# The first expert's rows are loaded before the last unit's scatter, and that unit's rows are added in PSUM

## The chip, the cores and the metric

One NeuronCore of a Trainium2 chip runs the whole program as one launch. The metric is the device time of one execution in microseconds; lower is better. Engines: PE (TensorE: products), DVE (VectorE), ACT (ScalarE), POOL (GpSimd, which also issues the indirect DMAs) and SP (SyncE, which issues most DMAs). Each engine works through its own instructions in the order of the program.

## The reference

Three layers in a row, all in float32:

```python
for t in range(768):                    # attention, 4 x 8 heads of width 40
    y[:, :, t] = r_t @ state
    Sa = state @ a_t
    state = state * w_t - outer(Sa, b_t) + outer(v_t, k_t)
x = y as 3072 tokens x 320
expert = argmax(x @ w_gate)             # 8 experts, 3072 / 8 * 2 = 768 rows each at most
gate = softmax(x @ w_gate)[expert]
x = gate * (relu(x_rows @ w1[expert]) @ w2[expert])     # F = 1024
out = elu(x @ w_in) @ w_out             # 2048 wide
```

A token's place in its expert's list is its rank among the tokens of that expert, counted in the order of the tokens.

## The kernel before

**Two halves.** `attention` works through 24 units of 128 tokens (64 steps of two batches). Each unit ends in one block of 128 rows of x, 320 wide. `ffn` follows it, with tile pools of its own in the memory that attention's pools leave: first the eight experts, then six blocks of 512 sorted tokens through the last layer.

**The table between them.** `disp` lies in DRAM: for each expert, 448 rows of 329 numbers (320 of x, the token's number, 8 logits of the gate). It is filled with zeros early. For a unit u the steps at its end are: `x` (line 558: product XT with IW on PE, copy into the tile XO on ACT, logits and token number on DVE), `b` (route: argmax as a 0/1 row, on DVE), `j` (line 592: ranks by two small products on PE, then the row numbers into `slot` on DVE) and `D` (line 609: an indirect DMA from POOL that scatters the 128 rows of XO into `disp`; a small memset follows it).

**The order.** What each engine gets is the order in which the Python program emits it. Attention's steps are generators; each letter of `ORDER`, and of what `slot(k)` returns for the units from 5 on, advances one of them. `V` advances the conversion of the last layer's weights from float64 to float32, in pieces: load on SP, integer and float operations on DVE (lines 858 to 870), store to `w32` on SP. Behind the last slot come, by hand: x and b of unit 23, six products that only keep PE busy (`warm`), j of unit 23, its scatter D, and the rest of V.

**The start of the experts.** `experts` (line 1192) splits the second half of the first expert's weights (`split`, lines 775 and 780: a copy on ACT gives the high part, four products on POOL for each of four quarters give the low part). Then `start` (line 917) loads the rows of expert 0, 448 rows as 112 partitions by 4, with one DMA on SP (line 1087), does 26 busy products, and turns the rows with twelve transposes into three PSUM banks (line 935). `prep` makes the high and low parts XH, XL and XS of them on ACT and DVE (lines 954 and 955). `fetch(2)` then loads the next weights on SP (lines 801 and 803).

**The steps of an expert.** Each expert has 8 steps f of 128 hidden columns. A step is `s1` (line 970: eight products of 448 columns into one of four PSUM banks), `relu` one step later (H on ACT, line 1100, and the remainder L on DVE, line 1101) and `s2` three steps later (lines 1035 to 1045: eight products). Between them, `extra(b, f)` puts other work: a cast of a quarter of later weights on ACT (the next weight load is issued in steps 0 and 4, as soon as the buffer that it refills has been read), conversion pieces with their loads (`more`), the next expert's rows (load in step 0, softmax of the gate in steps 2 and 3, turned in steps 4 to 6), and for expert 0 alone `late_gate` (line 1257). Its gate is worked out from the logits in the loaded rows and laid on the output columns, since the rows are turned without it: softmax before step 0 and in step 2, the products of line 1263 in step 3, a copy in step 4.

Of the kernel before, what the change touches and what calls it, by code (L numbers as in the profile page):

```python
# [33 lines left out]
ORDER = """
se1 sa0 se0 se0 v1 sc0 e0.0 sv se1 e0.1 sd p0 sw p0 e1.0 sw a0 p0 v0 p1 sa1 sx a0 p1 lw sz st1 e2.0 c0.0 a1
p2 p2 a1 c0.0 e1.1 sr1 Z7 c0.1 p1 e3.0 c0.1 k0.0 k0.1 c0.1 c1.0 e2.1 a2 a2 c1.0 p3 c1.1 k1.1 k1.0 c1.1 k1.0 e4.0 d1 k1.1
c1.1 e3.1 m0.0 l0 m0.1 k0.1 p2 p3 a3 l1 a3 p4 p4 p3 m1.1 c2.1 e5.0 k2.1 c2.0 c2.1 m1.0 r0 c2.0 k2.0 k0.0 a4 m2.1 a4 p5
st0 k2.0 k3.1 sc1 c3.0 c2.1 c3.1 ss1 k3.0 e4.1 m2.0 p4 r0 r1 c4.0 i0 e6.0 k3.0 n0 k3.1 m3.0 k4.1 p5 n1 o0 c3.1 p6
c3.0 e5.1 a5 a5 c3.1 m3.1 k2.1 r1 e7.0 l2 p5 k4.1 c4.1 k4.0 m4.1 e6.1 c4.0 c5.1 k5.1 l3 p6 k5.0 c5.0 c4.1 p7 c4.1 p6 a6
m5.0 a6 v2 v3 p7 c5.0 t1 m4.0 t0 c6.1 m6.1 c5.1 k4.0 f1 k6.1 c5.1 k6.0 k6.1 m5.1 sr0 a7 i1 c6.0 f1 f0 a7 o1 e7.1 e8.0 f1 f0  # L40
k5.0 p7 c6.1 f0 f1 f1 p8 c6.0 d0 e9.0 f0 k5.1 c7.1 f0 f1 f1 c6.1 c7.0 f0 f0 e8.1 c7.1 g1 c7.0 g0 p8 m7.0 a8 ss0 p8 m7.1
g0 k7.1 l5 l4 g1 k7.0 k7.1 g0 k8.0 g0 c7.1 l6 p9 e9.1 g1 a8 u0 m6.0 p9 k6.0 k8.1 u0 g1 l7 c8.0 k7.0 m8.0 c8.1 n2 t2 e10
w0 a9 p9 f2 n3 k8.1 a9 q0.0 w0 q0.1 q0.1 w0 i2 u1 u1 f2 q0.0 c8.0 f2 p10 k9.1 c9.1 f2 c8.1 c9.0 m8.1 k8.0 Z2 c8.1 f2 w0
Z4 p10 t3 f2 s0 k9.1 p10 c9.1 c9.0 w1 w1 k9.0 y0 f2 i2 k9.0 g2 s0 w1 e11 s0 c9.1 f3 k10.1 Z3 r2 a10 w1 a10 f3 k10.1 m9.0
f3 y0 m9.1 k10.0 p11 Z0 r2 c10.0 q1.0 q1.0 c10.1 x0 f3 p11 h2 q1.1 s1 f3 g2 a11 k10.0 m10.1 i2 f3 c10.0 g2 q1.1 c10.1 h2
e12 v4 p11 f3 s1 c10.1 x0 y1 y1 d2 g3 p12 a11 s1 k11.1 c11.0 x1 g3 r3 Z6 c11.0 g2 g3 p12 k11.1 h3 x1 m11.0 a12 Z5 p12 x0 r3
u2 a12 c11.1 c12.0 u2 g3 w2 d3 c11.1 w2 k11.0 w2 x1 k12.1 h3 q2.0 q2.1 Z1 b0 w2 c11.1 c12.1 u3 c12.1 m10.0 m11.1 s2 j0
o2 u3 w3 k11.0 q2.1 q3.1 c12.0 e13 z2 q2.0 s2 w3 y2 s2 l11 j0 l10 y2 t4 m12.0 m12.1 r4 v5 l9 g4 d4 w3 k12.1 r4 p13 D0
h4 x2 l8 g4 c12.1 k12.0 D1 h4 t5 q3.0 p13 w3 g4 g4 g4 s3 u4 x2 a13 l12 s3 z3 q3.0 u4 w4 w4 a13 q3.1 p13 i3 w4 g5 h5 y3
d5 x2 w4 y3 s3 s4 i3 k12.0 e14 t6 s4 s4 h5 v6  # L50
"""
FIRST = [f for f, n in GROUPS if f > 6]
AHEAD = (17, 19, 20, 21, 22, 23)

CV0, CVN = 17, 7


def slot(k):
    L = []
    a = lambda x: L.extend(x.split())  # L60
    live = k < NU

    nx, up = k + 1, k + (8 if k < 7 else 9)
    ups = up < NU
    pair = k - 3 if k % 2 else None
    work = {f - 6 + i: (g, i) for g, (f, n) in enumerate(GROUPS) for i in range(4) if f > 8}
    work[5] = (3, 3)
    w = work.get(k)
    if live: a(f"r{k} r{k}")
    if ups and k != 7: a(f"c{up}.0")  # L70
    if FU <= k < NU: a(f"g{k} g{k}")
    more = ups and up + 1 < NU
    if ups and k != 7: a(f"m{up}.0 c{up}.0")
    if more and k != 7: a(f"p{up+1}")
    a(f"x{k-2} x{k-2} x{k-2}")
    if k == NU: a(f"b{NU-2}.1")
    if FU <= k < NU: a(f"g{k} g{k}")
    if w and w[1]:
        a(f"i{w[0]}")
        if w[1] == 3: a(f"o{w[0]}")  # L80
    if k % 2 == 0: a(f"D{k-3}")
    second = f"c{up}.1 m{up}.1 c{up}.1 c{up}.1 p{up+1} l{up}"
    if ups: a(second if k != 7 else f"a{up} a{up} c{up}.0 m{up}.0 c{up}.0 p{up+1}")
    if k + 2 < NU: a(f"v{k+2}")
    V = (lambda: a("V")) if CV0 <= k < NU else (lambda: None)

    if nx in FIRST: a(f"t{nx}")
    a(f"q{k-1}.0 q{k-1}.0")
    V()
    if w and not w[1] and k != 6: a(f"i{w[0]}")  # L90
    if live: a(f"u{k} u{k}")
    if k == 7: a(second)
    if more: a(f"p{up+1}")
    a(f"q{k-1}.1 q{k-1}.1")
    V()
    if pair is not None: a(f"b{pair}")
    if ups:
        a(f"k{up}.0 k{up}.0 k{up}.1 k{up}.1")
    if FU <= nx < NU and nx not in FIRST: a(f"g{nx}")
    if live and k < 22: a(f"w{k} w{k} w{k} w{k}")  # L100
    if up + 2 < NU: a(f"E{up+2}")
    if more: a(f"a{up+1} a{up+1}")
    a(f"z{k-1}")
    if nx < NU: a(f"h{nx} h{nx}")
    if nx < NU: a(f"d{nx}")
    if k + 2 < NU and k + 2 not in FIRST: a(f"t{k+2}")
    if live and k < 22: a(f"s{k} s{k} s{k}")
    if k == NU: a(f"j{NU-2}.1 j{NU-2}.1 D{NU-2}")
    a(f"y{k-1} y{k-1}")
    if nx in FIRST: a(f"g{nx}")  # L110
    V()
    if pair is not None: a(f"j{pair} j{pair} D{pair}")
    if k == 6:
        up += 1
        a(f"c{up}.0 m{up}.0 c{up}.0 c{up}.1 m{up}.1 c{up}.1 c{up}.1 p{up+1} l{up} i{w[0]}")
        a(f"k{up}.0 k{up}.0 k{up}.1 k{up}.1 E{up+2} p{up+1} p{up+1}")
    return " ".join(L)


def attention(tc, nc, e_in, v_tok, d_in, wg, disp, xt, cst, ring, early, early_w, cv, cap):  # L120
# [548 lines left out]
    for k in range(KR, NU + 1):  # L669
        for key in slot(k).split():  # L670
            go(key)
        for _ in range(AHEAD.count(k)):
            next(early, None)
        if k == 8:
            zero_x()
# [816 lines left out]
```

## Time and profile before

| | |
|---|---|
| Median of 3 runs | 1051.43 us (1046.94 to 1054.29) |
| The profiled execution | 1045.15 us |
| Its span, first to last instruction | 1043.3 us |
| Mean granted clock of PE | 0.942 of 2.4 GHz |
| Busy: PE, DVE, POOL, ACT | 92%, 70%, 59%, 49% of the span |
| DMA | 121.67 MB, mean 117 GB/s |

Times in the views are microseconds from the span's start. A timeline names an engine's instructions with their start, duration and line; instructions of the same form that follow one another are one row with a count. The bracket at the end is the engine's idle time before it and what ended that. The granted clock is 1.00 at 2.4 GHz and 0.50 at 1.2 GHz. The chain of waits is followed back from the last instruction: at each step to what released it.

### The profile page before, as it was taken

How to read it: one execution, taken by the hardware profiler on the slowest of the kernel's cores; microseconds unless marked ns; L12 is line 12 of the kernel's file. 1: busy time of each engine (PE TensorE's matmuls, PEld its weight loads, DVE VectorE, ACT ScalarE, POOL GpSimd, SP SyncE). 2: the span in 40 equal slices, each digit the busy share in tenths (PEclk: the TensorE clock that was granted, in tenths of full speed). 3: DMA queues.
4: the chain of work that ended last, by engine and by line, in shares of the span. 5: the costliest groups of instructions: out<-in, count | busy, mean ns of one | idle time of the engine just before them, and what ended most of it. 6: DMA issues, size and time to landing. Idle time of an engine off the chain costs nothing.

```text
span 1043.3 us, 25335 instructions
## 1 busy us (share of the span) xinstructions
PE 959.6 (92%) x9995; PEld 868.6 (83%) x9995; DVE 726.0 (70%) x1287; ACT 515.7 (49%) x1011; POOL 616.3 (59%) x926
## 2 busy tenths in 40 slices
PE   4868978899899999989999999999999999999993
PEld 4858878798788889778888888888999889998893
DVE  8956757788674568547677777586767777677761
ACT  3646535566464334254445556465545555455551
POOL 4767929899898813377768777944333323333332
PEclk8867878899899889999999999999999999999997
DMA  6768776666665674386786766601001010100000
GB/s 163 170 171 201 167 135 124 146 138 137 131 122 117 138 192 116 118 227 192 224 225 169 225 192 206 226 24 26 26 1 52 1 26 26 26 26 1 26 2 28
DMA packets 180935, 121.67 MB, mean 117 GB/s; under 512 B 105744, under 2 KB 166824, under 8 KB 179176
## 3 DMA queue, kind: packets, MB, share of 16 engines
q1 hardware_dynamic: 176740, 102.89, 39.7%
q0 software_dynamic: 3168, 11.14, 3.1%
q10 hardware_dynamic: 900, 5.93, 2.3%
q8 instruction: 81, 1.33, 0.6%
q14 instruction: 46, 0.38, 0.1%
HBM read 86.87 MB, written 33.05 MB: 115 GB/s over the span
## 4 chain that ended last, share of the span: by engine, by line
PE 40%; DVE 7%; DMA 3%; ACT 3%; issue 2%; POOL 1%; SPq 0%; POOLq 0%; ACTq 0%; DVEq 0%
PE ph L970 21%; PE po L998 5%; PE po L997 5%; PE po L996 5%; DMA w<-E 2%; DVE L L1101 2%; DVE E L859 1%; ACT X L1094 1%; ACT ring L775 1%; DVE M L865 1%; DMA ring<-in_w_dram 1%; DVE N L864 1%; POOL L L1115 1%; ACT H L1100 1%; PE po L1037 1%
## 5 line engine op out<-in xcount | busy, mean ns | idle before, releaser
L780 POOL TENSOR_TENSOR ring<-ring,ring 128x64 fp32r<-128x64 f32 (+2 forms) x320 | 203.9, 674 | 75.3 <-ACT ring L775 75.3
L1115 POOL TENSOR_TENSOR L<-E,H 128x512 fp32r<-128x512 f32 x66 | 90.7, 1374 | 169.7 <-ACT H L1114 155.9
L970 PE MATMUL ph<-XH,ring 128*128 128x512 f32 (+1 forms) x640 | 170.5, 388 | 0.6 <-ACT XH L954 0.3
L1108 ACT ACTIVATE E<-N 128x512 f32<-128x512 f32 x96 | 60.8, 633 | 151.1 <-DVE N L1107 78.2
L353 POOL TENSOR_TENSOR X<-X,ring 128x60 f32<-128x60 f32 (+19 forms) x170 | 125.5, 738 | 13.3
L970 PEld LDWEIGHTS ph<-XH,ring 128*128 128x128 f32 x640 | 115.7, 189 | 14.7 <-ACT XH L954 0.6
L998 PE MATMUL po<-ring,L 128*128 128x320 f32 x384 | 119.4, 311 | 1.5 <-POOL L L1115 1.5
L996 PE MATMUL po<-ring,H 128*128 128x320 f32 x384 | 118.5, 309 | 0.2 <-ACT H L1114 0.2
L997 PE MATMUL po<-ring,H 128*128 128x320 f32 x384 | 118.5, 309 | 0.0
L970 PE MATMUL ph<-XL,ring 128*128 128x512 f32 (+1 forms) x320 | 96.7, 383 | 0.0
L970 PE MATMUL ph<-XS,ring 128*128 128x512 f32 (+1 forms) x320 | 96.5, 382 | 0.0
L351 POOL TENSOR_TENSOR ring<-X,ring 128x60 f32<-128x60 f32 (+19 forms) x108 | 69.8, 646 | 39.4 <-DMA ring<-dab 18.3
L1112 DVE SCALAR_TENSOR_TENSOR M<-E,M 128x512 f32<-128x512 f32 x96 | 79.4, 827 | 14.8 <-ACT M L1109 14.7
L1107 DVE TENSOR_SCALAR N<-ph 128x512 f32<-128x512 f32 x96 | 65.7, 684 | 27.9 <-PE ph L970 27.6
L996 PEld LDWEIGHTS po<-ring,H 128*128 128x128 f32 x384 | 72.1, 188 | 4.5 <-ACT H L1114 0.5
L997 PEld LDWEIGHTS po<-ring,H 128*128 128x128 f32 x384 | 71.9, 187 | 4.3
L998 PEld LDWEIGHTS po<-ring,L 128*128 128x128 f32 x384 | 72.1, 188 | 2.0 <-POOL L L1115 2.0
L1113 DVE SCALAR_TENSOR_TENSOR E<-ph,M 128x512 f32<-128x512 f32 x96 | 66.4, 691 | 8.1 <-DVE M L1112 0.5
L970 PEld LDWEIGHTS ph<-XL,ring 128*128 128x128 f32 x320 | 60.8, 190 | 10.9
L1101 DVE SCALAR_TENSOR_TENSOR L<-ph,H 128x448 fp32r<-128x448 f32 x64 | 39.4, 617 | 43.5 <-ACT H L1100 43.4
L970 PEld LDWEIGHTS ph<-XS,ring 128*128 128x128 f32 x320 | 60.2, 188 | 10.5
L775 ACT CAST ring<-ring 128x704 fp32r<-128x704 f32 x80 | 61.4, 778 | 12.4 <-DMA w<-GE 5.7
(238 smaller groups left out, 2166.9 us busy)
## 6 DMA issues: line engine op xcount, KB each, us to landing
ring<-in_w_dram SPq DMA_DIRECT2D x16, 640.0 KB
ring<-in_w_dram SPq DMA_DIRECT2D x32, 256.0 KB
RVU<-in_d_in_dram SPq DMA_DIRECT2D x48, 160.0 KB
dab<-AB SPq DMA_DIRECT2D x24, 256.0 KB
ring<-in_e_in_dram ACTq DMA_DIRECT2D x18, 321.6 KB
ring<-w SPq DMA_DIRECT2D x4, 1408.0 KB
disp<-ring SPq DMA_DIRECT2D x8, 575.8 KB
X<-disp SPq DMA_DIRECT2D x8, 575.8 KB
```

The costliest lines, as they stand in the source:

```text
L351: nc.gpsimd.tensor_tensor(tv, X[:, 0:n, s:s + 1].to_broadcast([128, n, m]), N[:, s:s + 1, s + 1:e].to_broadcast([128, n, m]), op=ALU.mult)
L353: nc.gpsimd.tensor_tensor(X[:, 0:n, s + 1:e], X[:, 0:n, s + 1:e], tv, op=ALU.subtract)
L775: s.nc.scalar.copy(B[:, 0:704], r)
L780: s.nc.gpsimd.tensor_tensor(B[:, to], r[:, q], B[:, q].bitcast(F32), op=ALU.subtract)
L970: nc.tensor.matmul(p, l, r[:, 0:s.T], start=i == 0, stop=i == len(seq) - 1)
L996: nc.tensor.matmul(o, H[:, c], hb, start=f == 0, stop=False)
L997: nc.tensor.matmul(o, H[:, c], lb, start=False, stop=False)
L998: nc.tensor.matmul(o, L[:, c], hb, start=False, stop=f == s.W.nf - 1)
L1107: nc.vector.tensor_scalar(N, p, 0.0, None, op0=ALU.min)
L1112: nc.vector.scalar_tensor_tensor(out=M, in0=E, scalar=1.0, in1=M, op0=ALU.add, op1=ALU.mult)
L1113: nc.vector.scalar_tensor_tensor(out=E, in0=p, scalar=0.0, in1=M, op0=ALU.max, op1=ALU.add)
L1115: eng.tensor_tensor(L, E, H.bitcast(F32), op=ALU.subtract)
```

## The change

The XO tile of unit 23 gets a place of its own that outlives attention. Its scatter moves out of attention to the start of `ffn`, behind the load of expert 0's rows, which is now four DMAs, one for each quarter. Rows of unit 23 that belong to expert 0 are therefore still zero in what is loaded. They are added by products: `oh` is 1 where column c is the row number of the token on that partition, and x of unit 23 (a high part and a remainder, 321 columns wide) times `oh` is accumulated in the three PSUM banks. The loaded rows are added behind it, by plain products with the identity in place of transposes. The busy products become 10 in place of 26. Expert 0's logits are loaded from the table by a DMA of their own in step 2; softmax follows in steps 4 and 5, the gate's products in step 6 and the copy in step 7.

The order of attention's steps is written out in `ORDER` in place of `slot` (which goes, with `KR`, `FIRST`, `AHEAD` and `CV0`). It is the same sequence except for its end:

```
before: q23.0 q23.0 q23.1 q23.1 z23 j22.1 j22.1 D22 y23 y23 | x23 b23.1 warm(6) j23.1 D23 V
after:  q23.0 q23.0 q23.1 V j22.1 q23.1 z23 j22.1 D22 V y23 V y23 | x23 b23.1 warm(6) j23.1
```

```diff
@@ attention
-        XO = wk.tile([128, RW], F32, tag="XO", name="XO", bufs=4)
+        XO = cst["xo"] if u == NU - 1 else wk.tile([128, RW], F32, tag="XO", name="XO", bufs=3)
...
-    do( f"j{NU-1}.1", f"D{NU-1}", "V")
+    do(f"j{NU-1}.1")
...
+    return sent
@@ Block.start
-        def start(s, busy=0):
-            for _ in s.load(True):
-                pass
+        def start(s, busy=0, add=None):
+            if not add:
+                for _ in s.load(True):
+                    pass
...
+            if add:
+                oh, parts = add
+                w = [slice(128 * k, 128 * k + (128, 128, s.W2)[k]) for k in range(3)]
+                for k, c in enumerate(w):
+                    for j, x in enumerate(parts):
+                        nc.tensor.matmul(P[k][0:c.stop - c.start, 0:s.T], x[:, c], oh[:, 0:s.T], start=j == 0, stop=False)
+                for i in range(4):
+                    for k, c in enumerate(w):
+                        nc.tensor.matmul(P[k][0:c.stop - c.start, s.P * i:s.P * i + s.P], s.X[0:s.P, i, c], ident[0:s.P, 0:s.P], start=False, stop=i == 3)
+            else:
+                for i in range(4):
+                    for k in range(3):
+                        s.turn(P[k], i, k)
@@ rows
-            nc.sync.dma_start(out=s.X[0:112], in_=src)
+            for i in range(4) if now else (slice(0, 4),):
+                nc.sync.dma_start(out=s.X[0:112, i], in_=src[:, i])
@@ experts
+        add = None if dyn else last_rows(bl[0])
         go(split(1), 5)
-        bl[0].start(0 if dyn else 26)
+        bl[0].start(0 if dyn else 10, add)
...
+    def last_rows(B):
+        xo = cst["xo"]
+        it = ap.tile([128, 512], F32, tag="N", name="N")[:, 0:SL]
+        oh, xh, xl = (ap.tile([128, 512], F32R, tag="H", name="H", bufs=6) for _ in range(3))
+        w = slice(0, D + 1)
+        nc.gpsimd.iota(it, pattern=[[1, SL]], base=SL, channel_multiplier=0, allow_small_or_imprecise_dtypes=True)
+        nc.scalar.copy(xh[:, w], xo[:, w])
+        nc.gpsimd.tensor_tensor(xl[:, w], xo[:, w], xh[:, w].bitcast(F32), op=ALU.subtract)
+        for _ in B.load(True):
+            pass
+        x = nc.gpsimd.indirect_dma_start(
+            out=disp, out_offset=bass.IndirectOffsetOnAxis(ap=cst["slot"][:, 23:24], axis=0),
+            in_=xo, in_offset=None).ins
+        for y in sent_x:
+            tc.declare_no_dep(x, y, reason="scatters write different rows")
+        f = ap.tile([128, 1], F32, name="sf", bufs=1)
+        nc.vector.tensor_copy(f, cst["slot"][:, 23:24])
+        nc.vector.tensor_scalar(oh[:, 0:SL], it, f, None, op0=ALU.is_equal)
+        return oh, (xh, xl)
+
     def late_gate(B):
-        g = yield from soft(B, "late")
+        yield
+        lg = ap.tile([128, 4, 8], F32, name="lgx", bufs=1)[0:112]
+        with nc.allow_non_contiguous_dma("the logits of a row"):
+            nc.sync.dma_start(out=lg, in_=dv[0, 1][:, :, D + 1:RW])
+        yield
+        yield
+        g = yield from soft(B, "late", lg)
```

## Rows read from the trace of the kernel before

**Rows 1.** Busy time by stage, 450 to 680: PE, PEld, DVE, ACT, POOL, clock, DMA, GB/s.

```profile
450.00:680.00 230.00, 225.08 (x1126) 199.40 (x1126) 167.45 (x310) 118.28 (x219) 176.66 (x275) 1.00 0.69 207
```

**Rows 2.** The chain of waits, 439 to 443: start, duration, what.

```profile
439.02 3.06 DMA disp<-XO,SLOT
...
442.47 0.34 SPq L1087
```

**Rows 3.** Timeline of PE, 447 to 472: start, duration, operation, shape, count, [idle <-releaser].

```profile
447.31 1.71 PE L935 MATMUL pt<-ident,X 112*128 112x112 f32 x12 [3.13 <-DMA X<-disp]
449.31 1.92 PE L970 MATMUL ph<-XH,ring 128*128 128x448 f32 x4 [0.29 <-ACT XH L954]
...
452.08 0.98 PE L970 MATMUL ph<-XH,ring 128*128 128x448 f32 x4
...
453.77 1.07 PE L970 MATMUL ph<-XH,ring 128*128 128x448 f32 x4
...
458.74 1.04 PE L1263 MATMUL pgate<-ident,g 112*128 112x112 f32 x8
...
471.06 1.05 PE L970 MATMUL ph<-XH,ring 128*128 128x448 f32 x4
```

**Rows 4.** Busy time by stage, 449 to 451; third column from the end: granted clock.

```profile
449.00:451.00 2.00, 1.71 (x5) 1.46 (x5) 1.62 (x3) 1.11 (x3) 2.00 (x4) 0.50 1.08 289
```

**Rows 5.** Timeline of DVE, 431 to 472.

```profile
431.51 1.28 DVE L530 TENSOR_TENSOR Qs<-q,mask 128x512 f32<-128x512 f32 x2
...
433.76 0.69 DVE L556 TENSOR_TENSOR XT<-y,GE 104x512 f32<-104x512 f32 x1 [0.40 <-PE y L552]
...
438.31 0.48 DVE L867 TENSOR_TENSOR GE<-GE,GE 128x320 f32<-128x320 f32 x1
...
439.06 0.49 DVE L870 SCALAR_TENSOR_TENSOR GE<-GE,GE 128x320 f32<-128x320 int32 x1
...
456.36 0.17 DVE L1074 TENSOR_REDUCE g<-X 112x4 f32<-112x32 f32 x1
...
457.08 0.17 DVE L1078 TENSOR_REDUCE g<-x 112x4 f32<-112x32 f32 x1
...
457.88 0.13 DVE L1342 COPY cnt<-pc 128x8 f32<-128x8 f32 x1
...
468.79 0.42 DVE L858 TENSOR_SCALAR N<-S 128x512 int32<-128x512 int32 x1
...
471.70 0.61 DVE L1101 SCALAR_TENSOR_TENSOR L<-ph,H 128x448 fp32r<-128x448 f32 x1
```

**Rows 6.** Timeline of POOL, 439 to 452.

```profile
439.02 0.96 POOL L610 DMA_INDIRECT disp<-XO,SLOT  x1 [3.92 <-issue]
...
442.78 0.10 POOL L1418 MEMSET one<- 128x8 f32 x1 [2.69 <-issue]
...
443.30 8.35 POOL L780 TENSOR_TENSOR ring<-ring,ring 128x64 fp32r<-128x64 f32 x16
```

**Rows 7.** Timeline of the SP queue, 451 to 457.

```profile
451.77 0.34 SPq L1087 DMA_DIRECT2D X<-disp  x1
452.21 2.29 SPq L801 DMA_DIRECT2D ring<-in_w_dram  x4
...
455.19 1.29 SPq L822 DMA_DIRECT2D S<-in_w_in_dram  x2
```

**Rows 8.** Busy time by stage, 453 to 465; the last two columns are DMA share, GB/s.

```profile
453.00:463.00 10.00, 10.00 (x56) 8.96 (x55) 5.90 (x22) 6.42 (x13) 6.76 (x14) 1.00 1.06 307
463.00:465.00 2.00, 1.73 (x11) 1.44 (x10) 1.55 (x4) 1.53 (x3) 1.77 (x3) 1.00 0.00 0
```

**Rows 9.** The scatters' landing times, from the view of the tile disp.

```profile
DMA to landing us min/median/max: 2.7/4.8/7.6
```

**Rows 10.** Timeline of ACT, 464 to 466.

```profile
464.33 0.79 ACT L775 CAST ring<-ring 128x704 fp32r<-128x704 f32 x1
465.01 0.56 ACT L1100 ACTIVATE H<-ph 128x448 fp32r<-128x448 f32 x1
```

More of the change, by code (lines that the diff above doesn't have):

```diff
@@ L39 @@
[L39 to L43, printed above, removed]
@@ L49 @@
-h4 x2 l8 g4 c12.1 k12.0 D1 h4 t5 q3.0 p13 w3 g4 g4 g4 s3 u4 x2 a13 l12 s3 z3 q3.0 u4 w4 w4 a13 q3.1 p13 i3 w4 g5 h5 y3
-d5 x2 w4 y3 s3 s4 i3 k12.0 e14 t6 s4 s4 h5 v6
-"""
[L52 to L117, printed above, removed]
@@ new lines @@
+se1 sa0 se0 se0 v1 sc0 e0.0 sv se1 e0.1 sd p0 sw p0 e1.0 sw a0 p0 v0 p1 sa1 sx a0 p1 lw sz st1 e2.0 c0.0 a1 p2 p2 a1 c0.0 e1.1 sr1 Z7 c0.1 p1 e3.0
+c0.1 k0.0 k0.1 c0.1 c1.0 e2.1 a2 a2 c1.0 p3 c1.1 k1.1 k1.0 c1.1 k1.0 e4.0 d1 k1.1 c1.1 e3.1 m0.0 l0 m0.1 k0.1 p2 p3 a3 l1 a3 p4 p4 p3 m1.1 c2.1 e5.0
+k2.1 c2.0 c2.1 m1.0 r0 c2.0 k2.0 k0.0 a4 m2.1 a4 p5 st0 k2.0 k3.1 sc1 c3.0 c2.1 c3.1 ss1 k3.0 e4.1 m2.0 p4 r0 r1 c4.0 i0 e6.0 k3.0 n0 k3.1 m3.0 k4.1
+p5 n1 o0 c3.1 p6 c3.0 e5.1 a5 a5 c3.1 m3.1 k2.1 r1 e7.0 l2 p5 k4.1 c4.1 k4.0 m4.1 e6.1 c4.0 c5.1 k5.1 l3 p6 k5.0 c5.0 c4.1 p7 c4.1 p6 a6 m5.0 a6 v2 v3
@@ new lines @@
+k21.1 g13 w12 w12 w12 w12 E23 a22 a22 z11 h13 h13 d13 t14 s12 s12 s12 y11 y11 r13 r13 c22.0 g13 g13 m22.0 c22.0 p23 x11 x11 x11 g13 g13 i5 o5 c22.1
+m22.1 c22.1 c22.1 p23 l22 v15 q12.0 q12.0 u13 u13 p23 q12.1 q12.1 b10 k22.0 k22.0 k22.1 k22.1 g14 w13 w13 w13 w13 a23 a23 z12 h14 h14 d14 t15 s13 s13
+s13 y12 y12 j10 j10 D10 r14 r14 c23.0 g14 g14 m23.0 c23.0 x12 x12 x12 g14 g14 D11 c23.1 m23.1 c23.1 c23.1 p24 l23 v16 q13.0 q13.0 i6 u14 u14 q13.1
+q13.1 k23.0 k23.0 k23.1 k23.1 g15 w14 w14 w14 w14 z13 h15 h15 d15 s14 s14 s14 y13 y13 r15 r15 g15 g15 x13 x13 x13 g15 g15 i6 v17 t16 q14.0 q14.0 u15
@@ L120, in attention @@
+j20 D20 A x22 x22 x22 b22.1 D21 q23.0 q23.0 q23.1 V j22.1 q23.1 z23 j22.1 D22 V y23 V y23
+"""
+CVN = 7
 def attention(tc, nc, e_in, v_tok, d_in, wg, disp, xt, cst, ring, early, early_w, cv, cap):
@@ L637, in attention @@
                  n=m_load, t=tt_load, f=t32, g=t64, r=rhs, u=u_solve, w=vu_tr, s=s_update, h=s_tr, q=q_mm, z=y_state, y=y_mm, x=x_out,
-                 b=route, j=route_mm, D=scatter, Z=zero_d, V=lambda: cv.pieces(spare, CVN))
+                 b=route, j=route_mm, D=scatter, Z=zero_d, X=zero_x, V=lambda: cv.pieces(spare, CVN))
     def spare(i, words):
@@ L652, in go @@
     def go(key):
+        if key == "A":
+            next(early, None)
+            return
         if key not in open_:
@@ L668, in attention @@
         go(key)
[L669 to L675, printed above, removed]
     for _ in early:
@@ L699, in consts @@
     c["cap"] = p.tile([128, 2], I32, name="CAP")
+    c["xo"] = p.tile([128, RW], F32, name="XL23")
     return c
@@ L883, in ahead, with ffn @@
     W.fetch(1)
-def ffn(tc, nc, cst, disp, xt, w1, w2, w32, out, ring, W0, cv):
+def ffn(tc, nc, cst, disp, xt, w1, w2, w32, out, ring, W0, cv, sent_x):
     ident = cst["ident"]
@@ L925, in start @@
             P = [ps.tile([128, 512], F32, tag="ph", name="pt") for _ in range(3)]
-            for i in range(4):
-                for k in range(3):
-                    s.turn(P[k], i, k)
+            if add:
[11 more added lines that the diff above has]
+                        s.turn(P[k], i, k)
             for _ in s.prep(P):
@@ L1067, in prep, with soft @@
                 yield
-    def soft(s, tag="s"):
+    def soft(s, tag="s", lg=None):
         t = lambda nm, sh: ap.tile(sh, F32, tag=tag + nm, name=nm, bufs=1)[0:112]
         g, x = t("g", [128, 4]), t("x", [128, 4, 8])
-        lg = s.X[0:112, :, D + 1:RW]
+        lg = s.X[0:112, :, D + 1:RW] if lg is None else lg
         nc.vector.tensor_reduce(g, lg, axis=AX.X, op=ALU.max)
@@ L1463, in network @@
         W0, cv = expert(nc, ring, w1, w2, 0), Convert(nc, w_in, w_out, w32)
-        attention(tc, nc, e_in, v_tok, d_in, wg, disp, xt, cst, ring, ahead(W0), W0, cv, cap)
-        ffn(tc, nc, cst, disp, xt, w1, w2, w32, out, ring, W0, cv)
+        sent = attention(tc, nc, e_in, v_tok, d_in, wg, disp, xt, cst, ring, ahead(W0), W0, cv, cap)
+        ffn(tc, nc, cst, disp, xt, w1, w2, w32, out, ring, W0, cv, sent)
 def layout(r, k, v, w, a, b, moe_w_gate, moe_w1, moe_w2, moe_capacity, moe2_w_in, moe2_w_out):
```

38 lines of the change are left out of this document (28 added, 10 removed).

## The prediction, made before the change was run

> **What bounds the kernel now.** I read the busy time by stage first. From 450 to 680 us PE works 225.08 of 230 us at the full clock [rows 1], so a later start of that stretch, or a wait inside it, is time added at the end, and an earlier start is time won if nothing inside takes it back. The open place is the seam between the two halves. The chain of waits gives it in order: the last unit's scatter starts at 439.02 and lands 3.06 us later, at 442.08; the load of the first expert's rows is issued at 442.47 [rows 2]. PE waits 3.13 us for that load, turns the rows from 447.31 to 449.02 and starts the first expert's products at 449.31; the next steps start at 452.08 and 453.77 [rows 3]. The first step thus takes 2.77 us and the second 1.69 us for the same eight products: from 449 to 451 the granted clock is 0.50, the 1.2 GHz level [rows 4]. What the change can reach is this seam, some 8 us of a 1043 us span.
>
> **Unit 23 gets about 1 us later.** The last three conversion operations on DVE (438.31 to 439.55, 1.24 us) move ahead, between the two evacuations that start at 431.51. XT, which needs the second one, waits 0.40 us for PE today [rows 5]; only that idle time covers any of it. The cost is between 0.84 and 1.24 us; I take 1.0. The last DVE work of unit 23, over at 438.31 today, then ends at 439.3.
>
> **The row load leaves earlier, but not at the landing of unit 22's scatter.** The memset of line 1418 has nothing to do with the dispatch table, and yet it starts only at 442.78, 0.70 us after unit 23's scatter has landed [rows 6]. I read this as: the first tiles of the second half wait for all of the first half. So the load's issue moves from 442.47 to 439.3 + 0.39 = 439.7, the 0.39 being the distance from landing to issue [rows 2]. Four issues of 0.34 take the place of one. The flight is 4.84 us today (442.47 to 447.31), shared with weights; the least is the scatter's 3.06. The last piece lands between 442.8 and 445.5; I take 444.0, 3.3 us earlier.
>
> **PE gets more work in front of the first step.** xh is one ACT copy, beside the rest. On POOL come 0.70 us of waits and 0.52 us of fills, as today (442.78 to 443.30), then the iota and xl. The split's sixteen products (176 columns each by the code) take 8.35 us, 0.52 each [rows 6]; by width xl is 0.95, and the iota between 0 and 1.3, where I take 0.6. That makes 442.1. The 0/1 matrix is one DVE operation beside it, 0.6 us like the one at 471.70 [rows 5]. Six products of 448 columns at 1.69 / 8 = 0.21 us each end at 443.5, about when the rows land. Then twelve products by the identity replace twelve turns: four such cost 1.04 us in line 1263, so twelve cost 3.1 us against 1.71 [rows 3]. The earlier pieces are worked on while the last one flies, so this ends near 446.6, and the first step starts at 446.9, 2.4 us earlier. The fewer warming products cost nothing: they lie ahead of the wait for the rows. With the 3.13 us of idleness gone I expect the clock to stay up, which gives 2.77 - 1.69 = 1.1 us (the other end is nothing). Head start: 3.5 us, between 2.4 and 4.
>
> **What is queued behind the moved scatter.** On POOL the scatter must now wait until the rows have landed, since it writes the table that they are read from. It starts at 444.0 + 0.7, its issue takes 0.96, and behind it stand the sixteen products of the weight split, 8.35 us [rows 6]. They end at 454.0 in place of 451.65. SP's next weight load refills the buffer that they read: issued at 452.21 today, 0.56 us after them [rows 7], it goes to 454.6.
>
> **The gate's logits become a transfer of their own.** Today they are columns of the rows already in SBUF. Now a small load is issued on SP in step 2, behind the weight load and the two conversion loads of step 1. Today that part of the queue lasts from 452.21 to 456.48, 4.27 us [rows 7], so the small load is issued at 458.9. From 453 to 463 the DMA engines are full and move 3.07 MB, and from 463 to 465 nothing [rows 8]: all that was issued from 451.77 on is through 10.8 us after 452.21. The next expert's rows (0.59 MB, 1.9 us at 307 GB/s) now go ahead of this burst, which leaves 8.9 us: the burst ends at 463.5, and the logits land at 464.5, one microsecond after it. Bounds: the shortest scatter flight, 2.7 us after issue, gives 461.6; the longest, 7.6, gives 466.5 [rows 9].
>
> The Trainium skill, DMA: Bandwidth & Descriptors, section Queues, rings and completion order, speaks against the change here: on each DMA engine descriptors are consumed in ring order, so 14 KB stand behind 2.5 MB. By that rule the landing is 464.5 and the sum +1.0; if the small load overtook the large ones it would be 461.6 and the sum -1.9. No row of this trace shows a small load behind a large one.
>
> **From the logits back to PE.** In step 4 the softmax of the gate comes ahead of the weight cast on ACT, and both ahead of step 4's relu. After the landing follow: softmax, first part, 0.72 (456.36 to 457.08), cast 0.79, relu 0.56 [rows 10], remainder 0.61, the next rows' remainder 0.61, softmax, second part, 0.80 (457.08 to 457.88), the conversions 2.91 (468.79 to 471.70), step 5's remainder 0.61 [rows 5]. The sum is 7.6: step 5 is through at 472.1. The products of a step take one of four PSUM banks. The gate's products move from step 3 to step 6 and take a bank that step 7 had; by my count step 7 then takes that of step 5, free at 472.1. Today step 7 starts at 471.06 [rows 3].
>
> **The sum.** Head start -3.5, wait in front of step 7 +4.5: 1.0 us later, between -1.9 (logits at 461.6) and +3.0 (at 466.5). Against the profiled execution's 1045.15 this is 1046.2; that execution lies 6.3 us under the median of the runs. Laid on the median, 1051.43, it is 1052.4.
>
> **Rivals.** (1) The head start is kept. If the four banks turn another way, so that step 7 does not need step 5's, only the last turn of the next rows waits, for step 4's remainder: 464.5 + 0.72 + 0.79 + 0.56 + 0.61 = 467.2, earlier than it is needed today. For it: PE waits little inside the stretch [rows 1]. Against it: DVE and ACT work in order, and both stop at the softmax. Time: -3.5 with the gate's 1.04 us still to come, about -2.5, up to -3.5 if the logits come early; 1048.9.
> (2) Slower: POOL is the bound. If the rows land at 445.5, the split ends at 455.5, the weight load leaves at 456.1, the small load at 460.4, and with the longest flight, 7.6 us, the logits land at 468.0; step 7 starts at 475.6, +4.5: 1056. It decides from a landing of the logits past 466 on. For it: POOL works without a gap through its 8.35 us. Against it: two late ends at once.
> (3) The change does not do what it says: the rows leave no sooner, because unit 22's scatter, for which they must wait, has a flight like the longest (7.6) and lands only near 442. Then four issues and the longer products are pure cost: the first step starts at 449.9, the scatter and all behind it 3 us later still than forecast, +4: 1055.5. Against it: the scatter at 439.02 needed 3.06 [rows 2].
>
> **How the numbers follow.** Forecast 0.53, rival 1 0.29, rival 2 0.10, rival 3 0.05, something else 0.03. The runs before scatter from 1046.94 to 1054.29. The range reaches from rival 1's best end, 1047.9, less 2 for that scatter, to rival 2: 1046 to 1056. One per cent, what a measurement of this kernel can tell from no change, is 10.5 us, more than the whole seam; no case reaches it on either side. Faster by over 1% 0.03, within 1% 0.94, slower 0.03, the small ends for what no row shows.
>
> **What would show it.** The first X load issued near 439.7 and landed near 444, the first step's product near 447, the clock at 1.00 from there. Right on the giving back: DVE idle in front of the late softmax, released by the logits' DMA, and a PE wait at step 6 or 7 of the first expert. Wrong: no such PE wait, or a start of the first step before 445 or after 449. Were the medians more than 6 us apart, something outside the seam would have moved, and the whole reading would be wrong.

## The result, and the profile after

| | before | after |
|---|---|---|
| Median | 1048.92 us (6 runs, 1045.71 to 1054.29) | 1061.83 us (6 runs, 1058.09 to 1069.91) |
| Ratio | | 1.0121, 95% interval 1.0074 to 1.0168 |
| The profiled execution, its span | 1045.15, 1043.3 us | 1058.09, 1056.4 us |
| Mean granted clock | 0.942 | 0.944 |

The change costs about 13 us, not 1. Most of that was lost more than 200 us ahead of the seam that the prediction worked on.

**Where it was lost.** First the copies of unit 5's x into XO, on ACT. The timeline of ACT in the kernel before (start, duration, line, operation, [idle <-releaser]):

```profile
198.53 0.43 ACT L567 COPY XO<-x 128x320 f32<-128x320 f32 x1
```

and after:

```profile
206.83 0.43 ACT L523 COPY XO<-x 128x320 f32<-128x320 f32 x1 [9.46 <-DMA disp<-XO,SLOT]
```

The view of the tile `disp` after the change has a line that the kernel before lacks (waiter: us, times), and POOL's timeline has the scatter that unit 5's copy waits for, unit 2's:

```profile
  ACT XO L523: 14.7, 4
```

```profile
203.29 1.03 POOL L566 DMA_INDIRECT disp<-XO,SLOT  x1 [0.30 <-issue]
```

In the kernel before, the same scatter stands at the same place:

```profile
203.36 1.03 POOL L610 DMA_INDIRECT disp<-XO,SLOT  x1 [0.30 <-issue]
```

With three buffers unit 5 writes into the one that unit 2 used; with four it is unit 1's, whose scatter is issued at 137.12 in the kernel before. After the change unit 2's scatter stands on POOL behind the products of `solve`, which follow one another until 202.07, and is issued at 203.29, so the copy, and everything that ACT has behind it, waits until the rows have left the buffer. Three more such waits, 5.2 us together, follow at units 8, 9 and 11. The slip is never made up. Unit 22's and unit 23's x products on PE, before:

```profile
428.52 1.12 PE L562 MATMUL x<-IW,XT 128*128 128x88 f32 x8 [0.43 <-DVE XT L556]
...
434.50 1.12 PE L562 MATMUL x<-IW,XT 128*128 128x88 f32 x8 [0.79 <-DVE XT L556]
```

and after:

```profile
439.09 1.12 PE L518 MATMUL x<-IW,XT 128*128 128x88 f32 x8 [0.44 <-DVE XT L512]
...
446.06 1.12 PE L518 MATMUL x<-IW,XT 128*128 128x88 f32 x8 [0.79 <-DVE XT L512]
```

Unit 22 is 10.57 us late. Unit 23 follows it after 6.97 us instead of 5.98: the conversion operations in front of it cost 0.99.

**The seam after**, to be laid against [rows 3, 6, 7]. Timeline of PE:

```profile
452.38 1.47 PE L886 MATMUL pt<-H 128*128 128x448 f32 x6 [0.29 <-issue]
453.69 2.70 PE L889 MATMUL pt<-ident,X 112*128 112x112 f32 x24
456.60 1.32 PE L935 MATMUL ph<-XH,ring 128*128 128x448 f32 x4 [0.21 <-ACT XH L919]
...
463.63 1.08 PE L935 MATMUL ph<-XH,ring 128*128 128x448 f32 x4 [1.20 <-DVE L L1067]
...
469.65 1.08 PE L935 MATMUL ph<-XH,ring 128*128 128x448 f32 x4 [2.50 <-DVE L L1067]
...
484.82 1.79 PE L935 MATMUL ph<-XH,ring 128*128 128x448 f32 x4 [1.61 <-DVE L L1067]
```

The wait of 3.13 us for the rows is gone. Three waits have come in its place, ahead of steps 3, 4 and 7: 5.31 us. Timeline of POOL:

```profile
454.87 1.00 POOL L1235 DMA_INDIRECT disp<-XL,SLOT  x1 [2.84 <-DMA X<-disp]
455.89 12.57 POOL L734 TENSOR_TENSOR ring<-ring,ring 128x64 fp32r<-128x64 f32 x24
```

POOL waits for the rows, scatters (the tile apart is called XL in the views), and then works without a gap until 468.46: the sixteen products of the split and eight of the next weights. Timeline of SP (the first column is the issue):

```profile
450.15 1.76 SPq L1053 DMA_DIRECT2D X<-disp  x4
...
461.12 0.35 SPq L1053 DMA_DIRECT2D X<-disp  x1
464.31 2.22 SPq L755 DMA_DIRECT2D ring<-in_w_dram  x4
...
468.24 0.81 SPq L1250 DMA_DIRECT2D lgx<-disp  x1
```

Timelines of ACT and of DVE:

```profile
461.57 0.78 ACT L729 CAST ring<-ring 128x704 fp32r<-128x704 f32 x1 [2.63 <-DMA ring<-in_w_dram]
```

```profile
463.50 4.99 DVE L1327 CAST cf<-CAP 128x2 f32<-128x2 int32 x1
...
476.87 0.18 DVE L1039 TENSOR_REDUCE g<-lgx 112x4 f32<-112x32 f32 x1
...
480.94 0.41 DVE L812 TENSOR_SCALAR N<-S 128x512 int32<-128x512 int32 x1
...
483.23 1.00 DVE L819 SCALAR_TENSOR_TENSOR M<-S,N 128x512 f32<-128x512 uint32 x1
484.15 0.61 DVE L1067 SCALAR_TENSOR_TENSOR L<-ph,H 128x448 fp32r<-128x448 f32 x1
```

Busy time by stage after (PE, PEld, DVE, ACT, POOL; the last three columns are the granted clock, DMA share, GB/s), to be laid against [rows 1, 4]; the first row is the stretch of [rows 1], moved by 10.57:

```profile
460.57:690.57 230.00, 221.00 (x1099) 195.32 (x1099) 169.91 (x306) 116.27 (x215) 176.92 (x275) 0.99 0.67 204
...
457.00:470.00 13.00, 9.22 (x43) 7.31 (x43) 8.25 (x12) 3.41 (x7) 11.46 (x22) 1.00 0.66 194
478.00:483.00 5.00, 5.00 (x34) 4.60 (x32) 4.00 (x9) 3.08 (x6) 4.36 (x8) 1.00 0.72 188
485.00:489.00 4.00, 4.00 (x13) 3.57 (x14) 3.73 (x7) 3.50 (x7) 2.15 (x4) 0.58 0.84 199
```

Step 3 waits because step 0's relu stands on ACT behind a cast whose weights have not landed. Step 4 waits for step 1's remainder, which stands on DVE behind a cast of two numbers per partition that takes 4.99 us and ends with POOL's run. Step 7 waits for step 5's remainder at 484.15, behind the late softmax and the conversions. Behind that last wait the granted clock is 0.50, the 1.2 GHz level, from 485.2 to 488.2 (0.58 is the mean of four microseconds), where it was 1.00 ahead of it: from step 7 to the next expert it takes 4.92 us in place of 3.36. Behind the wait of 2.50 it stayed at 1.00. The chain of waits (start, duration, what) names the second and third of these:

```profile
463.58 4.92 DVE cf L1327
469.65 1.91 PE ph L935 x8
484.82 3.28 PE ph L935 x8
```

**One measure for all kernels.** The table gives the start of unit 23's x product from the span's start, its distance from unit 22's, and then, counted from it, the first expert's steps and the next expert's first step (starts in PE's timelines, subtracted; the last digit can be off by one). The distance from the next expert's first step to the first of the sorted blocks is no measure: it is 193.9 to 204.5 us across these single profiles, whose code differs little or not at all in that stretch.

| kernel | x of 23 | 22 to 23 | step 0 | step 4 | step 5 | step 7 | next expert |
|---|---|---|---|---|---|---|---|
| before | 434.50 | 5.98 | 14.81 | 25.05 | 29.20 | 36.56 | 39.92 |
| after | 446.06 | 6.97 | 10.53 | 23.59 | 28.72 | 38.75 | 43.67 |
| e1 three buffers | 448.78 | 5.98 | 15.39 | 26.29 | 29.94 | 37.24 | 40.60 |
| e2 rotate four | 431.66 | 6.97 | 10.50 | 23.43 | 28.67 | 38.68 | 42.03 |
| e3 capacity early | 439.13 | 6.97 | 10.93 | 20.87 | 27.68 | 38.80 | 42.18 |
| e4 weights early | 434.98 | 6.98 | 13.30 | 22.23 | 29.57 | 41.46 | 44.81 |
| e5 scatter between | 436.04 | 6.97 | 10.51 | 20.05 | 24.81 | 36.06 | 40.96 |
| e6 logits first | 440.20 | 6.98 | 10.50 | 20.16 | 25.71 | 34.32 | 37.67 |
| e7 six pieces | 434.48 | 5.89 | 11.41 | 20.67 | 25.78 | 34.00 | 37.34 |
| e8 old, six pieces | 435.37 | 5.98 | 14.04 | 24.78 | 28.85 | 36.20 | 39.53 |
| e9 one tile apart | 441.80 | 6.97 | 11.56 | 24.54 | 29.67 | 39.69 | 43.04 |
| e10 probe | 434.40 | 6.97 | 10.50 | 19.70 | 25.37 | 33.96 | 37.30 |

The three kernels with the old seam differ by 1.1 us in the last column. That is its uncertainty.

### The profile page after: what moved, and what is told of

It is laid out like the page before. It is cut to its first block, busy times and chain, and to the rows that moved or that the text cites. A ratio compares the mean times of both kernels' runs of the same rounds, so it can differ in the third digit from the quotient of the medians.

```text
span 1056.4 us, 25347 instructions
## 1 busy us (share of the span) xinstructions
PE 961.6 (91%) x9997; PEld 867.3 (82%) x9997; DVE 736.6 (70%) x1289; ACT 516.2 (49%) x1012; POOL 617.3 (58%) x927
## 4 chain that ended last, share of the span: by engine, by line
PE 50%; POOL 15%; DVE 12%; issue 10%; DMA 8%; ACT 3%; SPq 1%; POOLq 0%; ACTq 0%; DVEq 0%
PE ph L935 17%; POOL ring L307 6%; POOL X L309 5%; PE po L962 4%; PE po L963 4%; PE po L961 4%; PE q L481 3%; POOL L L1081 2%; DMA w<-E 2%; PE ut L425 2%; PE sc L233 2%; PE x L518 2%; DVE L L1067 2%; DMA TA<-dx 1%; DMA ring<-in_e_in_dram 1%
## 5 line engine op out<-in xcount | busy, mean ns | idle before, releaser
L309 POOL TENSOR_TENSOR X<-X,ring 128x60 f32<-128x60 f32 (+19 forms) x170 | 121.2, 713 | 13.3
L307 POOL TENSOR_TENSOR ring<-X,ring 128x60 f32<-128x60 f32 (+19 forms) x108 | 78.9, 730 | 41.1 <-DMA ring<-dab 21.3
L1080 ACT CAST H<-E 128x512 fp32r<-128x512 f32 x96 | 59.1, 616 | 14.8 <-DVE E L1079 12.1
```

What stands on the lines that cost most here:

```text
L307: nc.gpsimd.tensor_tensor(tv, X[:, 0:n, s:s + 1].to_broadcast([128, n, m]), N[:, s:s + 1, s + 1:e].to_broadcast([128, n, m]), op=ALU.mult)
L309: nc.gpsimd.tensor_tensor(X[:, 0:n, s + 1:e], X[:, 0:n, s + 1:e], tv, op=ALU.subtract)
```

## The experiments

### e1: the kernel before with three XO buffers

```diff
-        XO = wk.tile([128, RW], F32, tag="XO", name="XO", bufs=4)
+        XO = wk.tile([128, RW], F32, tag="XO", name="XO", bufs=3)
```

> The kernel before with one edit: three XO buffers in place of four. Theory (buffers): unit 5's XO copy waits on ACT for unit 2's scatter, which stands on POOL behind a solve; attention from unit 5 on is 8 to 10 us later, the copy at 198.5 goes to about 206.8, and the ratio to the kernel before is 1.008 to 1.010. Rival (layout or chance): the slip comes from the new tile that moves every later tile in SBUF, or from the scatter of the runs; then this kernel, which has no new tile, is at 1.000 within 0.004.

Measured: 1057.0 us, ratio 1.0075 (1.0049 to 1.0102). In the timeline of ACT unit 5's copy waits as it does after the change:

```profile
208.77 0.43 ACT L567 COPY XO<-x 128x320 f32<-128x320 f32 x1 [7.33 <-DMA disp<-XO,SLOT]
```

One number changed, nothing else, and some 8 us of the 13 are there, with an interval of 5 to 11; the rival had no loss.

### e2: the change with four XO buffers in rotation

Unit 23's own tile becomes one of four, used by every fourth unit.

```diff
-        XO = cst["xo"] if u == NU - 1 else wk.tile([128, RW], F32, tag="XO", name="XO", bufs=3)
+        XO = cst["xo"] if u % 4 == 3 else wk.tile([128, RW], F32, tag="XO", name="XO", bufs=3)
```

> The changed kernel, but the tile that outlives attention is used by every fourth unit, so that XO has four places again, in the same memory. Theory (buffers): unit 5's copy goes back to about 198.5 to 199 and attention's 10.6 us are won back; what is left is the seam, +2.5 us: ratio to the kernel before 1.001 to 1.004. Rival (layout): the tile still moves all others, so the slip stays: ratio 1.010 to 1.013.

Measured: 1047.53 us, ratio 1.0000 (0.9967 to 1.0033). The wait is gone:

```profile
198.04 0.42 ACT L523 COPY XO<-x 128x320 f32<-128x320 f32 x1
```

The seam is as after the change (the table: 10.50 at step 0, 38.68 at step 7). With e1 this settles the loss: it is the buffer that was taken out of the rotation. The memory is laid out as after the change, so the layout is not the cause. The seam by itself is no gain and no loss that the times can tell, which is to say within 3.5 us; the table has it 3.1 us later at the next expert (1.0 at unit 23 and 2.1 behind it).

### e3: e2 with the capacity's four operations ahead of the experts

```diff
...
+    capacity()
     ct = counts()
     experts(0, more=more)
```

`capacity` holds the four DVE operations that stood at the start of `counts`, the cast of 4.99 us first among them.

> As the kernel with four places, and the four small DVE operations on the capacity (the cast that took 4.99 us) are done ahead of the experts, before POOL's split begins. Theory (shared path): the cast waited because POOL worked without a gap from 455.89 to 468.46; done early it takes 0.5 us or less, step 1's remainder is 5 us earlier, the 2.50 us wait of PE ahead of step 4 goes; 1.5 to 2.5 us faster than the kernel with four places. Rival (weights): step 1 is held by the weight load that ACT's casts wait for, the slow cast only stood in its shadow; then less than 0.7 us is won and PE waits ahead of step 4 as before.

Measured: 1048.1 us, ratio 1.0001 (0.9973 to 1.0029). The cast takes 0.17 us there, and step 4 starts 2.6 us earlier than in e2; step 7 starts no earlier, and the 1.5 to 2.5 us that were expected are not there. Timelines of DVE, POOL and PE:

```profile
459.61 2.34 DVE L1040 TENSOR_TENSOR x<-X,g 112x32 f32<-112x32 f32 x1
```

```profile
449.90 12.62 POOL L734 TENSOR_TENSOR ring<-ring,ring 128x64 fp32r<-128x64 f32 x24
```

```profile
465.36 1.68 PE L900 MATMUL pt<-ident,X 112*128 112x112 f32 x4 [1.95 <-ACT X L1060]
...
477.93 1.09 PE L935 MATMUL ph<-XH,ring 128*128 128x448 f32 x4 [1.14 <-DVE L L1067]
```

The next small operation on DVE, in the softmax of the next expert's rows, now stands in the same place beside POOL's run. The wait moved on, to the turn of those rows and to step 7. Behind that turn the granted clock is 0.50 from 468 to 471, and from step 5 to step 6 it takes 5.20 us, for 3.65 after the change.

### e4: e3 with the next expert's first weights loaded ahead of the rows

```diff
 def ahead(W, more=None):
...
     W.fetch(1)
+    if more:
+        more.fetch(0)
...
-        fetch(2)
+        if dyn:
+            fetch(2)
```

> As the kernel with the early capacity, and the second expert's first weights are loaded right behind the first expert's last, ahead of the rows. Theory: ACT's wait of 2.63 us for these weights and PE's 1.20 us ahead of step 3 go, 1 to 2 us faster than with the early capacity alone; PE then waits only ahead of step 7, for step 5's remainder behind the conversions. Rival: the large load now stands in the queue in front of the rows and holds them back by 2 us or more; no gain.

Measured: 1050.69 us, ratio 1.0026 (0.9995 to 1.0057): no gain, as the rival had it. The waits of ACT for the weights and of PE ahead of step 3 are gone, as the theory had it, but step 0 starts at 13.30, and all steps behind it are 1.4 to 2.7 us later than in e3. The path is another than the rival's. The chain of waits (start, duration, what) has unit 22's scatter in front of the rows:

```profile
434.70 6.65 DMA disp<-XO,SLOT
```

It lands at 441.35, and the first load of the rows is issued only behind it, at 441.74: 6.8 us after unit 23's product, where e3 has 4.5. ACT, DVE and POOL wait for the same landing. Beside POOL's run the operation of e3's 2.34 us takes 5.78 here, and PE waits 2.48 us for the turn of the next rows. That the early load is what holds the scatter up is likely, and not shown.

### e5: e3 with two quarters of the split ahead of the scatter

```diff
         for _ in B.load(True):
             pass
+        go(quarters, 2)
         x = nc.gpsimd.indirect_dma_start(
...
```

> e3_capacity_early with one move: the first two quarters of the first expert's weight split go ahead of unit 23's scatter on POOL, in the hole of 3.37 us in which POOL waited for the rows (445.51 to 448.87 there). Nothing is left out. Theory (the head start is given back because POOL idles for the rows and everything on POOL and behind it is 3 us late): the scatter starts about 0.9 us later, the split ends about 3.3 us earlier, the third weight load leaves 3 us earlier, the small DVE operation of the next expert's softmax (2.34 us in e3) falls under 0.7, the 1.95 us wait ahead of the turn of the next rows falls under 0.5; counted from unit 23's x product, step 5 starts at 25 or earlier (27.68 in e3, 29.20 in the kernel before) and the sorted blocks start at 237.0 to 238.5 (239.97 in e3, 238.08 and 239.42 in two profiles of the old seam). Time 1.5 to 2.5 us under e3, ratio to before 0.997 to 0.999. Rival (the next expert's rows, which must wait for the scatter's landing, set step 5): the scatter 0.9 later makes those rows 0.9 later, step 5 starts at 28 to 29 and the sorted blocks at 240 to 241; no gain.

Measured: 1045.73 us, ratio 0.9981 (0.9955 to 1.0007). Timelines of POOL and PE:

```profile
441.94 4.36 POOL L734 TENSOR_TENSOR ring<-ring,ring 128x64 fp32r<-128x64 f32 x8
446.45 0.99 POOL L1237 DMA_INDIRECT disp<-XL,SLOT  x1 [0.15 <-issue]
447.48 8.40 POOL L734 TENSOR_TENSOR ring<-ring,ring 128x64 fp32r<-128x64 f32 x16
```

```profile
472.09 1.82 PE L935 MATMUL ph<-XH,ring 128*128 128x448 f32 x4 [2.51 <-DVE L L1067]
```

The scatter goes 0.7 us later against unit 23's product (10.41 for 9.74), and the third weight load 3.5 us earlier (issued at 15.67 for 19.21). Step 5 starts at 24.81, as the theory had it, where the rival had 28 to 29. Most of that is lost again at step 7, by the 2.51 us above, and behind it, where the granted clock is 0.50 from 472.4 to 475.0: step 5 is 4.4 us earlier than in the kernel before, step 7 is 0.5 earlier, the next expert 1.0 later. In front of the late softmax DVE idles 1.47 us, until the logits land (it starts on them at 464.48). The sorted blocks start at 234.9, earlier than either expected, but of the 5.1 us to e3 only 1.2 are there when the next expert starts; the rest lies in the stretch that is no measure.

### e6: e5 with the logits loaded first

```diff
     def late_gate(B):
-        yield
         lg = ap.tile([128, 4, 8], F32, name="lgx", bufs=1)[0:112]
```

> e5_scatter_between with the load of expert 0's logits issued on SP ahead of the next expert's rows and the conversion loads, and the gate's softmax in steps 3 and 4, its products in step 5 and its copy in step 6, one step earlier each. Nothing is left out. Theory (step 7 is late since the late softmax and the conversions stand ahead of step 5's remainder on DVE): the wait before step 7 (1.14 us in e3, 1.61 in the changed kernel) falls under 0.3, and the sorted blocks start 1.0 to 1.5 us earlier than in e5, counted from unit 23's x product. Rival (the gate's products take a bank wherever they stand): the wait moves to step 6 with the same size, and the next expert's rows leave 0.4 us later; the sorted blocks start 0 to 0.5 us later than in e5.

Measured: 1044.59 us, ratio 0.9944 (0.9917 to 0.9972): faster than the kernel before, and far from the interval of the changed one. The last wait of step 7, in PE's timeline:

```profile
474.53 1.07 PE L935 MATMUL ph<-XH,ring 128*128 128x448 f32 x4 [0.17 <-DVE L L1067]
```

Step 7 starts at 34.32 and the next expert at 37.67, 3.3 us earlier than in e5 and 2.3 earlier than before. Some 1.5 of the 3.3 are the clock, which is 1.00 from 475 to 479 here. So the wait at step 7 came from the late gate, whose load and softmax this edit moves together, and it did not move to step 6. The gain that was expected to show at the sorted blocks did not (234.97 for 234.89). The times gain 0.56%, some 5.9 us, more than the 2.3 - 1.0 = 1.3 us that the table gives (the next expert earlier, unit 23 later); the interval ends at 0.28%, 2.9 us. The same surplus stands in e2 to e5, whose times are 3.1 to 4.0 us better than their rows of the table, each within some 3 us. So it need not belong to this edit; what it is stays open.

### e7 and e8: one piece of the conversion less in attention

e7 is e6, e8 the kernel before, with the same edit (in e8 the first line reads `CV0, CVN = 17, 7`):

```diff
-CVN = 7
+CVN = 6
...
-        if (f not in (2, 3)) if b else f > 4 or f == 1:
+        if (f not in (2, 3) or b > 4) if b else f > 4 or f == 1:
```

> e6_logits_first with one piece of the last layer's weight conversion less in attention (six in place of seven; the seventh goes to the experts, whose conversion steps get two more places each from the sixth expert on). Nothing is left out. Theory (the conversion operations moved ahead of unit 23's last product cost it about 1 us): the distance from unit 22's x product to unit 23's falls by 0.8 to 1.3 us, the rest of the program from there keeps its length, and the ratio to before is 0.995 to 0.998. Rival (the operations were covered there, or the experts' DVE has no room for a 22nd piece): the distance stays within 0.3 us, or the start of the sorted blocks counted from unit 23's product moves back by 0.5 us or more, and the time is that of e6.

> The kernel before with the same one piece of the conversion less in attention and the same places among the experts: the control for e7_six_pieces. Nothing is left out. If the seam of the changed kernel is what gains in e7, this one stays within 0.2% of before, since the last piece stood behind the scatter there; if the freed DVE time in attention is what gains, it is faster by as much as e7 (0.3% or more).

Measured: e7 1041.84 us, ratio 0.9944 (0.9913 to 0.9974); e8 1043.63, ratio 0.9950 (0.9924 to 0.9975). In e7 unit 23 follows unit 22 after 5.89 us instead of 6.98: the term of 1.0 us is real, and comes from those operations. But e7 is no faster than e6, and the control, whose seam is the old one, gains as much as either. One piece less in attention is thus worth about 0.5% to the old kernel, for a reason that its seam does not show (its columns in the table are those of before within 0.9 us), and does not add to e6's gain. In e7's profile the rival's sign is there: the sorted blocks start 241.8 us after unit 23's product, for 235.0 in e6. DVE's timeline has the place, a remainder of the first sorted block:

```profile
655.39 10.99 DVE L1031 TENSOR_TENSOR XL<-X,XH 128x512 fp32r<-128x512 f32 x1
```

POOL works without a gap beside it, from 643.58 to 665.83; PE waits 4.2 us, and from 665 to 670 the granted clock is 0.50. In e8 the same operation takes 1.00 us. How many of e7's runs have this hold the record does not say: three of the eleven, the profiled one among them, take 1048.2 to 1050.1 us, the others 1037.3 to 1043.0. Where e8's gain comes from is open. What beats both kernels here is e6, and e7 and e8 as much, e8 without the change.

### e9: the change, with unit 5 alone in another tile

```diff
-        XO = cst["xo"] if u == NU - 1 else wk.tile(...)
+        XO = cst["xo"] if u in (5, NU - 1) else wk.tile(...)
```

> The changed kernel with its three XO buffers, where unit 5 alone writes its XO into the tile that unit 23 uses later, so that it no longer has to wait for unit 2's scatter; everything else as in the changed kernel. Nothing is left out. Theory (the slip of attention is one wait, unit 5's copy behind unit 2's scatter, and all later units only carry it on): unit 5's copy starts at 197 to 201 (206.8 in the changed kernel), ACT's waits for the scatters' landing fall from 14.7 us to under 6, and the time is that of the four buffers, ratio to before 0.998 to 1.002. Rival (three buffers are too few all along): the wait moves to units 6 to 9 and the ratio is 1.005 to 1.012.

Measured: 1054.06 us beside 1051.3 for before on that chip, ratio 1.0012 (0.9985 to 1.0040). Timeline of ACT, units 5 and 9:

```profile
199.34 0.43 ACT L523 COPY XL<-x 128x320 f32<-128x320 f32 x1
...
269.88 0.42 ACT L523 COPY XO<-x 128x320 f32<-128x320 f32 x1 [6.86 <-DMA disp<-XO,SLOT]
```

(XL is the tile apart.) One unit out of the rotation brings the time back to that of before within the interval. In the profile the wait is not simply gone: unit 9 now has one of 6.86 us, just above the theory's bound of 6, and unit 23 starts at 441.80, between the three buffers' 446.06 and 448.78 and the four's 431.66 to 440.20. Unit 5's wait is thus the larger part; what the one at unit 9 costs, the times do not tell.

### e10: a small cast set beside POOL's run

```diff
+            if b == 0 and f == 0 and not dyn:
+                q = ap.tile([128, 4], F32, name="probe", bufs=1)
+                nc.vector.tensor_copy(q[:, 0:2], cst["cap"])
+                nc.vector.tensor_copy(q[:, 2:4], cst["cap"])
```

> e6_logits_first with two more operations on DVE, in the first step of the first expert: the capacity, 128 x 2 integers in SBUF, is cast into a new tile, twice. They come while POOL works through sixteen products of a weight split without a gap (8.42 us in e6), with some 7 us of them still to go. Nothing else is changed; the two results are not used. Theory (a small DVE operation from SBUF to SBUF loses to POOL for as long as POOL's products follow one another without a gap): the first cast takes 5 to 8 us and ends within 0.6 us of the end of POOL's run, the second one 0.2, and the second step's remainder on DVE, steps 3 and 4 of the first expert come 2 to 4 us later than in e6. Rival (it waits for one product at most): the first takes 0.2 to 0.7 us, and nothing moves; then the long cast of the changed kernel had another cause.

Measured once: 1045.09 us. Timelines of DVE and POOL:

```profile
446.73 2.77 DVE L1214 CAST probe<-CAP 128x2 f32<-128x2 int32 x1
449.41 0.16 DVE L1215 CAST probe<-CAP 128x2 f32<-128x2 int32 x1
```

```profile
445.85 8.43 POOL L734 TENSOR_TENSOR ring<-ring,ring 128x64 fp32r<-128x64 f32 x16
```

Neither expectation holds. The cast is held for 2.6 us, five products, not one; but it ends at 449.50, not with the run at 454.28. Products of 8.43 / 16 = 0.527 us each put that end behind the seventh of the sixteen. What lets DVE in is left open. The eighth product is the last of one split, and the ninth needs a cast that ACT finishes only at 449.48; in the changed kernel, where ACT finished its part 0.1 us after the hold began, it lasted to the run's end. That would go with a hold for as long as POOL's next products stand ready. The kernel before speaks against so simple a rule: there the same cast, at 454.53, took 0.50 us in the middle of eight products. No run was made to tell these apart. Nothing behind the probe came later than in e6, since DVE's next operation, step 0's remainder, had to wait for ACT until 450.08 anyway.

## Why the prediction was wrong, point by point

- **The failed step: the XO buffer, costed at nothing without being costed.** The part "Unit 23 gets about 1 us later" takes in all that the change does to attention, and the diff's first line, four buffers to three and one apart, stands in none of the terms. e1 and e2 show what it was worth: 1.0075 alone, and with the fourth back 1.0000 where the change had 1.0121. The code and the trace before the change had the material: the scatters stand in POOL's order behind `solve`, and a buffer is free only when its scatter has landed. The question that was not asked is which unit's scatter frees the buffer of unit u, and when that scatter is issued. With three buffers it is unit 2's for unit 5. In the kernel before it is issued at 203.36, 4.8 us after the 198.53 at which unit 5's copy starts there. The slip is 8.3 us at unit 5 and 10.6 at unit 22.
- **The condition that I named held.** Medians over 6 us apart were to mean that something outside the seam had moved. They are 12.9 apart, and it had. The chance of 0.03 for slower by over 1% was far too small for a change with an edit left out of the sum.
- **Unit 23 later by 1.0: right** (0.99; taken away again in e7).
- **Rows earlier, POOL's wait, the scatter behind it: right.** Counted from unit 23's product, which I put at 435.5: step 0 forecast at 11.4, measured 10.53; scatter 9.2, measured 8.81; third weight load 19.1, measured 18.25. The clock stayed at 1.00 here; yet the first step took 2.34 us (456.60 to 458.94), not 1.69, since its remainders of x were ready only at 458.4. The gain there was 0.4 us of the 1.1.
- **The head start given back: right that it is, too small, and wrong in its place.** Forecast: all of it, and only in front of step 7, through logits that land late; the seam 1.0 us later in sum, 3.0 at most. Step 7 does start later than before, at 38.75 for the forecast's 36.6, and behind step 5's remainder as the count of the banks said. With unit 23's 1.0 the table has the seam 3.2 us later at step 7 and 4.7 at the next expert (3.1 in e2). DVE read the logits at 476.87 without a wait; they held nothing up. The giving back began before that, at steps 3 and 4, with weights that land late and a cast that POOL holds up, and the clock of 0.50 behind step 7's wait added 1.6 us (4.92 less 3.36). I had taken POOL's lateness into the weight load alone, and costed none of DVE's operations beside its run. Where the places in front were cleared, in e5, the forecast path does show: DVE idle for the logits, then PE waiting 2.51 us ahead of step 7.
- **The logits behind the burst.** After the change the logits' load shows no wait, so this trace does not say when they landed. In e3, e4 and e5 DVE waits for them, 0.67, 1.84 and 1.47 us. In e5 the load is issued at 455.85 and DVE starts on the logits at 464.48, when the DMA engines have moved 17 GB/s from 463 to 464 and nothing from 464 on: at the end of the burst, as the forecast took it. That agrees with the rule on ring order that the prediction takes from the Trainium skill (DMA: Bandwidth & Descriptors, section Queues, rings and completion order).
- **The rivals.** Head start kept (0.29) did not happen, and could have: e6 keeps 2.3 of its 4.3 us at the next expert, by moves on DVE, POOL and SP. POOL as the bound (0.10) is nearest to what the seam does, with its mechanism on DVE instead of in the weight load. Rival 3's path, rows held back by unit 22's scatter, shows in e4, with a flight of 6.65 us.
- **The range**, 1046 to 1056, would have held e2, e3 and e4, the seam without the lost buffer; e5, e6 and e7 lie under it. It was a range for the seam, and it was laid on a median of three runs, 1051.43, where six have 1048.92.

## What to carry to other kernels

A buffer count is part of the schedule: when one is taken out of a rotation, go to the unit whose last reader frees the buffer that each unit will now write, and look up when that reader runs, above all when it is a DMA in another engine's order. Where a wait is moved from one engine to another (here from PE to POOL), fill the hole with work that already stands behind it, as e5 does, before counting the gain (step 5 came 2.9 us earlier there; the time alone does not tell it from e3's). And when one stall goes, the next operation in the same queue meets the same cause; a removed stall is a gain only once the whole chain behind it has been read again.
